# Weights first, one pipeline for all tiles, queries turned one tile ahead

## Chip, cores, metric

One core of a Trainium2 chip runs the whole kernel. Its engines are named as in the profile: PE multiplies matrices (PEld are its weight loads), ACT is ScalarE, DVE is VectorE, POOL is GpSimd. The metric is device microseconds per execution. A ratio is the mean time of one kernel's fast runs over the mean of the other's fast runs from the same rounds, with a 95% interval; it is not quite the ratio of the medians that are quoted, which are over all runs. A run is called slow when it is over 1.5% above the fastest of its kernel.

## The reference

Eight batches of eight heads, 576 positions, 64 values each. Cosine-weighted linear attention, then an expansion with softplus and a projection back.

```python
r_q, r_k = max(q, 0), max(k, 0)              # times cos and sin of the position: q_p, k_p
kv  = einsum('bhsf,bhsd->bhfd', k_p, v)      # per head 128 x 64
z   = sum(k_p, axis=2)
x   = (q_p @ kv) / (q_p @ z + 1e-6)          # 4608 tokens x 512
out = softplus(x @ w_in) @ w_out
```

Both kernels replace softplus by its linear part, `h/2 + ln 2`, so that the two weight matrices fold into one (`W_c`) and a constant row. They measure the largest squared norms of x and of w_in at the end; if the linear part could be too coarse, an exact branch runs (it never does with these inputs).

## The kernel before

The tokens are 36 tiles of 128. A pair of batches has nine: four full ones for each, and one made of the last 64 positions of both. Each tile passes through these steps (shortened; "to turn" means to transpose by a matmul on PE):

```python
def turn_queries(b, n):            # PE transposes relu(q) times cos/sin, ACT copies it out
    ps = qt_ps.tile([128, 512], F32, tag="qt")           # two buffers
    for j, (hj, t) in enumerate(pair):
        nc.tensor.matmul(ps[...], q_r[:, hj, t], diag[:, t])
    nc.scalar.copy(dst, ps)                              # qT
def attend(n):                     # 8 matmuls, then DVE divides: den, rden, x
    ...
def turn_x(n):                     # PE transposes x, ACT copies it and sums its squares
    ...
    nc.scalar.copy(xT_all[:, n], ps)
    nc.scalar.activation(square, x, ACT.Square, bias=zero_b, accum_out=x_norm[:, n : n + 1])
def emit(n):                       # PE: x @ W_c, DVE adds the constant row, then stored
    ...
```

The loop over batch b runs all of this a few tiles apart. The turns in it are those of the *next* batch; nine turns are spread over four or five tiles, with what is left done in a burst at the end:

```python
for j, i in enumerate(mine):
    attend(i)
    ... scale_values(b + 1, hq, c)         # DVE
    if j == 2 and b + 2 < B:
        relu(b + 2)                        # POOL
    if more and j >= last - 1:
        key_values(b + 1, j - last + 1)
    some(1)                                # one turn of batch b + 1
    turn_x(i - 1)
    some(1 if j < last else 9)
    emit(i - 2)
```

Loads: q, k, v of batch 0, then the weights. While those arrive, four tiles of batch 0 are attended; then the weights are turned and folded, and the four are emitted.

## Time and profile before

| what | value |
|---|---|
| time, median | 150.5 us |
| span of the profile | 148.7 us |
| first attended tile | 17 us |
| weights folded, first emit | 42.9 us |
| steady state | 60 to 127 us |
| last output made | 141.2 us |
| busy share of the span: PE, DVE, ACT, POOL | 81%, 73%, 76%, 36% |

### The profile page before, as it was taken

Reading aid. Unit: us, or ns where it says so; the run is one execution under the profiler, and the core shown is the slowest. Engines: PE = TensorE matmul, PEld = TensorE weight load, DVE = VectorE, ACT = ScalarE, POOL = GpSimd, SP = SyncE. Lnnn points to the kernel's source line nnn. Section 1 sums busy time; section 2 is a strip of 40 time slices with the busy share of each in tenths; the row PEclk is TensorE's granted clock in tenths of the full one; section 3 lists DMA queues with packets and bytes.
Section 4 is the critical chain, followed back from the end, with each engine's and each line's share of the span. In section 5 each row is a group of like instructions: output and inputs, shape, how many; then the busy total and the mean of one; then the engine's idle time right before and its main releaser. Section 6 shows DMA issues by size and latency. Waiting matters only on the chain.

```text
span 148.7 us, 3802 instructions
## 1 busy us (share of the span) xinstructions
PE 119.9 (81%) x1482; PEld 75.6 (51%) x1482; DVE 108.9 (73%) x237; ACT 113.7 (76%) x255; POOL 53.0 (36%) x67
## 2 busy tenths in 40 slices
PE   6966875999967728798979899897899988999510
PEld 2323665444434507566657567575567755664100
DVE  6867494699467579978967986994998798599420
ACT  3468298999995626899899889989988989967300
POOL 6965132231300095196079059219009200000000
PEclk9999999999999986999999999999999999999985
DMA  1999999999999999999999999999942324144430
GB/s 21 181 179 216 213 213 202 209 204 209 207 207 208 267 266 209 208 208 265 239 250 256 239 239 269 228 256 249 241 171 82 142 74 109 61 155 152 153 90 4
DMA packets 20678, 28.07 MB, mean 189 GB/s; under 512 B 1200, under 2 KB 15536, under 8 KB 20656
## 3 DMA queue, kind: packets, MB, share of 16 engines
q0 software_dynamic: 15408, 18.35, 71.8%
q1 hardware_dynamic: 5248, 9.44, 18.8%
q8 instruction: 12, 0.20, 0.5%
q14 instruction: 10, 0.08, 0.2%
HBM read 36.70 MB, written 9.44 MB: 310 GB/s over the span
## 4 chain that ended last, share of the span: by engine, by line
PE 33%; DVE 25%; ACT 23%; issue 7%; DMA 5%; POOL 3%; DVEq 0%; POOLq 0%
PE o_ps L316 17%; DVE o_sb L318 11%; ACT square L367 9%; DVE vcs L213 8%; DMA v_sb<-in_v_dram 5%; PE kv_ps L227 5%; PE num_ps L279 4%; PE ps L252 4%; DVE x L289 3%; ACT square L303 3%; ACT qT L260 3%; ACT w_inT L152 3%; PE xT_ps L298 2%; ACT xT_all L301 2%; ACT kvblk L234 2%
## 5 line engine op out<-in xcount | busy, mean ns | idle before, releaser
L260 ACT CAST qT<-ps 128x512 bf16<-128x512 f32 x72 | 40.6, 592 | 11.3 <-PE ps L252 10.9
L316 PE MATMUL o_ps<-W_c,xT_all 128*128 128x512 bf16 x144 | 36.9, 378 | 5.1 <-DVE o_sb L318 3.5
L318 DVE TENSOR_TENSOR o_sb<-o_ps,b_bc 128x512 f32<-128x512 f32 x36 | 24.8, 688 | 13.4 <-PE o_ps L316 13.3
L252 PE MATMUL ps<-diag,q_r 128*128 128x256 bf16 x144 | 27.7, 279 | 8.1 <-ACT qT L260 4.6
L213 DVE TENSOR_TENSOR vcs<-v_sb,cs_wide 128x1152 bf16<-128x1152 bf16 x32 | 27.9, 871 | 2.4 <-ACT qT L260 1.2
L289 DVE TENSOR_TENSOR x<-num_ps,rden 128x512 bf16<-128x512 f32 x36 | 24.9, 692 | 3.3
L303 ACT ACTIVATE square<-x,zero_b 128x512 bf16<-128x512 bf16 x36 | 26.6, 739 | 0.0
L279 PEld LDWEIGHTS <-qT 128*128 128x128 bf16 (+1 forms) x320 | 19.6, 101 | 9.0 <-DVE x L289 1.9
L279 PE MATMUL num_ps<-kvblk,qT 128*128 128x130 bf16 (+1 forms) x320 | 23.4, 223 | 0.6 <-ACT kvblk L234 0.5
L301 ACT CAST xT_all<-xT_ps 128x512 bf16<-128x512 f32 x36 | 21.5, 596 | 3.0 <-PE xT_ps L298 3.0
L316 PEld LDWEIGHTS <-xT_all 128*128 128x128 bf16 x144 | 13.8, 97 | 17.1 <-issue 7.9
L252 PEld LDWEIGHTS <-q_r 128*128 128x128 bf16 x144 | 11.8, 99 | 15.0 <-issue 8.0
L234 ACT CAST kvblk<-kv_ps 64x260 bf16<-64x260 f32 x32 | 12.0, 375 | 6.0 <-PE kv_ps L227 5.7
L298 PE MATMUL xT_ps<-perm,x 128*128 128x128 bf16 x128 | 12.6, 222 | 3.0 <-DVE x L289 1.2
L160 PE MATMUL wc_ps<-w_out_sb,w_inT 128*128 128x512 bf16 x64 | 14.0, 379 | 0.1
L192 POOL TENSOR_SCALAR q_r<-q_sb 128x1152 bf16<-128x1152 bf16 x12 | 13.6, 1145 | 0.0
L298 PEld LDWEIGHTS <-x 128*128 128x128 bf16 x144 | 10.8, 99 | 5.3 <-issue 2.1
L227 PE MATMUL kv_ps<-vcs,k_sb 64*64 64x132 bf16 x576 | 11.5, 219 | 2.1 <-DVE vcs L213 2.0
L187 POOL TENSOR_SCALAR k_sb<-k_sb 128x2304 bf16<-128x2304 bf16 x6 | 12.6, 2102 | 0.0
L73 POOL DMA_DIRECT2D k_sb<-in_k_dram x9 | 6.7, 739 | 16.1 <-PE kv_ps L227 10.7
L367 ACT ACTIVATE square<-w_inT,zero_b 128x512 bf16<-128x512 bf16 x16 | 11.6, 723 | 0.5
L335 POOL COPY gate<-vcs 128x2 bf16<-128x2 bf16 x6 | 1.1, 190 | 29.1 <-DVE vcs L213 29.1
(55 smaller groups left out, 115.4 us busy)
## 6 DMA issues: line engine op xcount, KB each, us to landing
out_dram<-o_sb SPq DMA_DIRECT2D x32, 256.0 KB, 5.9
q_sb<-in_q_dram POOLq DMA_DIRECT2D x7, 576.0 KB, 20.5
k_sb<-in_k_dram POOLq DMA_DIRECT2D x7, 576.0 KB, 18.5
v_sb<-in_v_dram POOLq DMA_DIRECT2D x7, 576.0 KB, 20.9
xT_all<-in_moe_w_in_dram POOLq DMA_DIRECT2D x4, 512.0 KB, 12.6
w_out_sb<-in_moe_w_out_dram POOLq DMA_DIRECT2D x4, 512.0 KB, 18.5
out_dram<-o_sb SPq DMA_DIRECT2D x8, 128.0 KB, 4.0
q_sb<-in_q_dram POOLq DMA_DIRECT2D x2, 288.0 KB, 5.0
```

Source lines behind the costliest of these rows:

```text
L213: nc.vector.tensor_mul(view(vcs, [T * 2 * VW + 2, 2], [2 * VW, T], [1, D], offset=2 * hq * T * 2 * VW + c * VW), kqv[b, "v"][:, 2 * hq : 2 ...
L227: nc.tensor.matmul(kv[64 * i : 64 * i + 64, h2, : 2 * VW], k_r[rows, 2 * hq + i, t, :], vcs[rows, 2 * hq + i, t, :, :], start=(t == 0), st ...
L252: nc.tensor.matmul(ps[:, 256 * j : 256 * j + 256], q_r[:, hj, t, :, :], diag[:, t, :, :], start=True, stop=True, skip_group_check=True,)
L260: nc.scalar.copy(dst, ps.rearrange("p (j c s) -> p j c s", j=2, c=4))
L279: nc.tensor.matmul(num[p0 : p0 + m, g, :C], qTs[b][:, hq, 2 * c + h2, t0 : t0 + m], blk_bufs[b % 3][:, h2, hq, c, :], start=(c == 0), stop ...
L289: nc.vector.tensor_mul(x, view(num, [256, 4], [66, 2], [1, D]), view(rden, [2, 4], [1, 2], [0, D]))
L298: nc.tensor.matmul(ps[:, g, :], x[:, g, :, :], perm if len(tiles[n]) == 1 else ident, start=True, stop=True, skip_group_check=True,)
L301: nc.scalar.copy(xT_all[:, n], ps)
L303: nc.scalar.activation(square, x, ACT.Square, bias=zero_b, accum_out=x_norm[:, n : n + 1])
L316: nc.tensor.matmul(ps, xT_all[:, n, g, :], W_c[:, g, :], start=(g == 0), stop=(g == 3))
L318: nc.vector.tensor_add(o_sb, ps, b_bc)
L367: nc.scalar.activation(square, w_inT[:, ft, :], ACT.Square, bias=zero_b, accum_out=w_norm[:, ft : ft + 1])
```

## The change

The intent is plainness and balance: weights come first, in eight blocks that are turned, squared and folded as they land; every tile then passes through one loop; two tiles share one ACT instruction for the norms; and only the queries of the next tile are turned ahead, two turns per tile with no burst. The core (loads, constants, the end and the head's order are cut):

```diff
-    for ko in range(KO):
-        nc.gpsimd.dma_start(w_in_sb[:, ko, :], moe_w_in[ko * 128 : (ko + 1) * 128, :])
...
+    for j in range(1, BLOCKS):
+        load_w(j)                       # 256 columns of w_in, 256 rows of w_out
+    for name in ("k", "v", "q"):
+        for part in range(2):
+            load(0, name, part)
...
-        nc.scalar.activation(square, x, ACT.Square, bias=zero_b, accum_out=x_norm[:, n : n + 1])
...
+        for i in mine:
+            left = mine[-1] - i
+            if more and left in (1, 2):
+                scale_values(b + 1, 2 - left)
             attend(i)
+            if more and left == 1:
+                pool_relu(b + 1)
+            ahead = list(turns.get(i + 1, []))
+            if ahead:
+                turn_queries(*ahead.pop(0))
+            if more and left < 2:
+                key_values(b + 1, 1 - left)
+            if i >= 1:
                 turn_x(i - 1)
+                if i % 2 == 0:
+                    square(view(xs.pop(i // 2 - 1), [1, 2 * D_MODEL]), 2 * D_MODEL, ...)
+            if ahead:
+                turn_queries(*ahead.pop(0))
+            if i >= 2:
                 emit(i - 2)
```

More of the change, by code (lines that the diff above doesn't have):

```diff
@@ L75, in load, with fetch, load_w @@
         )
-    warm = singles.tile([128, 512], BF16)
+    def fetch(b):
+        for name in ("k", "v", "q"):
+            load(b, name)
+    xT_all = singles.tile([128, N_TOK // 128, KO, 128], BF16)
+    w_in_sb = xT_all[:, -FO:].rearrange("p n g t -> p (n g t)").rearrange(
+        "p (ko f) -> p ko f", ko=KO
+    )
+    w_out_sb = singles.tile([128, FO, D_MODEL], BF16)
+    BLOCKS = 8
+    FB = FO // BLOCKS
+    w_in_r = moe_w_in.rearrange("(ko p) f -> p ko f", p=128)
+    w_out_r = moe_w_out.rearrange("(fo p) m -> p fo m", p=128)
+    def load_w(j):
+        cols = slice(128 * FB * j, 128 * FB * (j + 1))
+        nc.gpsimd.dma_start(w_in_sb[:, :, cols], w_in_r[:, :, cols])
+        nc.gpsimd.dma_start(w_out_sb[:, FB * j : FB * (j + 1), :], w_out_r[:, FB * j : FB * (j + 1), :])
+    warm = singles.tile([128, 2 * D_MODEL], BF16)
     nc.vector.memset(warm, 1.0)
-    load(0, "q", 0)
-    load(0, "q", 1)
+    load_w(0)
     idx_i = singles.tile([128, T], mybir.dt.int32)
@@ L87 @@
     make_identity(nc, ident)
-    for part in range(2):
-        load(0, "k", part)
-        load(0, "v", part)
-    xT_all = singles.tile([128, N_TOK // 128, KO, 128], BF16)
-    w_in_sb = xT_all[:, 4 : 4 + D_FF // 128].rearrange("p n g t -> p (n g t)").rearrange(
-        "p (ko f) -> p ko f", ko=KO
-    )
-    w_out_sb = singles.tile([128, FO, D_MODEL], BF16)
-    for ko in range(KO):
-        nc.gpsimd.dma_start(w_in_sb[:, ko, :], moe_w_in[ko * 128 : (ko + 1) * 128, :])
-    w_out_r = moe_w_out.rearrange("(fo p) m -> p fo m", p=128)
-    for f in range(0, FO, 4):
-        nc.gpsimd.dma_start(w_out_sb[:, f : f + 4, :], w_out_r[:, f : f + 4, :])
-    for b in (1, 2, 3):
-        for name in ("q", "k", "v"):
-            load(b, name)
+    for j in range(1, BLOCKS):
+        load_w(j)
+    for name in ("k", "v", "q"):
+        for part in range(2):
+            load(0, name, part)
+    for b in (1, 2):
+        fetch(b)
     ones = singles.tile([128, 128], F32)
     nc.vector.memset(ones, 1.0)
-    blk_bufs = []
-    for r in range(3):
-        blk = singles.tile([128, 2, 2, 2, C], BF16, name=f"kvblk{r}")
-        nc.vector.memset(blk, 0.0)
-        blk_bufs.append(blk)
     idx_f = singles.tile([128, T], F32)
@@ L123, with constants @@
     cs_wide = singles.tile([128, 2, T, D], BF16)
-    nc.scalar.copy(cs_wide, view(cs_col, [1, 2 * T], [0, D]))
     diag = singles.tile([128, T, 2, 128], BF16)
-    for t in range(T):
-        for c in range(2):
-            nc.vector.tensor_scalar_mul(diag[:, t, c, :], ident, cs_col[:, c, t : t + 1])
     perm = singles.tile([128, 128], BF16)
-    nc.vector.tensor_copy(view(perm, [2, 64], [1, 2]), view(ident, [1, 64], [64, 2]))
+    blk_bufs = [singles.tile([128, 2, 2, 2, C], BF16, name=f"kvblk{r}") for r in range(3)]
+    VW = D + 2
+    vcs_bufs = [singles.tile([128, 4, T, 2, VW], BF16, name=f"vcs{r}") for r in range(2)]
+    def constants():
+        nc.vector.tensor_copy(cs_wide, view(cs_col, [1, 2 * T], [0, D]))
+        for t in range(T):
+            for c in range(2):
+                nc.vector.tensor_scalar_mul(diag[:, t, c, :], ident, cs_col[:, c, t : t + 1])
+                yield
+        nc.vector.tensor_copy(view(perm, [2, 64], [1, 2]), view(ident, [1, 64], [64, 2]))
+        yield
+        for r in range(2):
+            for hp in range(4):
+                at = 0 if hp % 2 else D
+                nc.vector.tensor_copy(
+                    vcs_bufs[r][:, hp, :, :, at : at + 2], view(cs_col, [1, T], [T, 2], [0, 2])
+                )
+                yield
+        for r in range(3):
+            nc.vector.memset(blk_bufs[r], 0.0)
+            yield
     W_c = singles.tile([128, KO, D_MODEL], BF16)
@@ L134, with turn_w_in, square, fold @@
     w_inT = singles.tile([128, FO, D_MODEL], BF16)
-    def turn_w_in(ko, half):
-        n = (2 * ko + half) % 3
-        pool, tag = (xt_ps, "xt") if n == 0 else (qt_ps, "qt")
-        ps = pool.tile([128, 8, 128], BF16, tag=tag, name="wT_ps")
-        for j in range(8):
-            ft = 8 * half + j
-            nc.tensor.matmul(
-                ps[:, j, :], w_in_sb[:, ko, ft * 128 : (ft + 1) * 128], ident,
-                is_transpose=True, start=True, stop=True, skip_group_check=True,
-            )
-        dst = view(
-            w_inT, [D_MODEL, 8], [128, 2], [1, 64],
-            offset=8 * half * D_MODEL + 256 * (ko // 2) + 64 * (ko % 2),
-        )
-        src = ps.rearrange("p f (h d) -> p f h d", h=2)
-        if half:
-            nc.scalar.copy(dst, src)
-        else:
-            nc.vector.tensor_copy(dst, src)
-    def fold(pair, quarter, ps):
-        for ft in range(4 * quarter, 4 * quarter + 4):
-            for j in range(2):
-                g = 2 * pair + j
+    w_norm = singles.tile([128, FO], F32)
+    x_norm = singles.tile([128, N_TOK // 256], F32)
+    def turn_w_in(j):
+        pool, tag = (xt_ps, "xt") if j % 3 == 0 else (qt_ps, "qt")
+        ps = pool.tile([128, FB, KO, 128], BF16, tag=tag, name="wT_ps")
+        for f in range(FB):
+            for ko in range(KO):
+                ft = FB * j + f
+                nc.tensor.matmul(
+                    ps[:, f, ko, :], w_in_sb[:, ko, ft * 128 : (ft + 1) * 128], ident,
+                    is_transpose=True, start=True, stop=True, skip_group_check=True,
+                )
+        for f in range(FB):
+            nc.vector.tensor_copy(
+                view(w_inT, [256, 2], [64, 2], [128, 2], [1, 64], offset=(FB * j + f) * D_MODEL),
+                view(ps, [256, 2], [128, 2], [64, 2], [1, 64], offset=f * D_MODEL),
+            )
+    def square(source, size, dst):
+        nc.scalar.activation(warm[:, :size], source, ACT.Square, bias=zero_b, accum_out=dst)
+    def fold(j, ps):
+        for ft in range(FB * j, FB * (j + 1)):
+            for g in range(KO):
                 nc.tensor.matmul(
-                    ps[:, j, :], w_inT[:, ft, g * 128 : (g + 1) * 128], w_out_sb[:, ft, :],
+                    ps[g // 2][:, g % 2, :], w_inT[:, ft, g * 128 : (g + 1) * 128], w_out_sb[:, ft, :],
                     start=(ft == 0), stop=(ft == FO - 1),
@@ L195, in relu_q, with pool_relu, scale_values @@
         )
-    VW = D + 2
-    vcs_bufs = []
-    for r in range(2):
-        vcs = singles.tile([128, 4, T, 2, VW], BF16, name=f"vcs{r}")
-        vcs_bufs.append(vcs)
-    def mark_values(r):
-        for hp in range(4):
-            at = 0 if hp % 2 else D
-            nc.vector.tensor_copy(
-                vcs_bufs[r][:, hp, :, :, at : at + 2], view(cs_col, [1, T], [T, 2], [0, 2])
-            )
-    def scale_values(b, hq, c):
-        vcs = vcs_bufs[b % 2]
-        nc.vector.tensor_mul(
-            view(vcs, [T * 2 * VW + 2, 2], [2 * VW, T], [1, D],
-                 offset=2 * hq * T * 2 * VW + c * VW),
-            kqv[b, "v"][:, 2 * hq : 2 * hq + 2],
-            view(cs_wide, [0, 2], [D, T], [1, D], offset=c * T * D),
-        )
+    gate = singles.tile([128, 2], BF16)
+    def pool_relu(b):
+        nc.gpsimd.tensor_copy(gate, vcs_bufs[b % 2][:, 3, T - 1, 1, VW - 2 :])
+        if b > 0:
+            for hq in range(2):
+                relu_q(b, hq, nc.gpsimd)
+        if b + 1 < B:
+            relu_k(b + 1, nc.gpsimd)
+    def scale_values(b, hq):
+        vcs = vcs_bufs[b % 2]
+        for c in range(2):
+            nc.vector.tensor_mul(
+                view(vcs, [T * 2 * VW + 2, 2], [2 * VW, T], [1, D],
+                     offset=2 * hq * T * 2 * VW + c * VW),
+                kqv[b, "v"][:, 2 * hq : 2 * hq + 2],
+                view(cs_wide, [0, 2], [D, T], [1, D], offset=c * T * D),
+            )
     def key_values(b, hq):
@@ L240, with turn_queries @@
     qTs = {}
-    TURNS = [(hq, tp) for tp in range(TP) for hq in range(2)] + [(0, TP)]
-    def turn_queries(b, n):
-        hq, tp = TURNS[n]
+    def turn_queries(b, tp, hq=0):
         q_r = q_rs[b]
-        if n == 0:
+        if b not in qTs:
             qTs[b] = work.tile([128, 2, 4, S], BF16, tag="qT", name="qT", bufs=3)
@@ L260, in turn_queries @@
         nc.scalar.copy(dst, ps.rearrange("p (j c s) -> p j c s", j=2, c=4))
-    tiles = []
+    tiles, turns = [], {}
     for b in range(B):
-        tiles += [[(b, 128 * tp, 128, 0)] for tp in range(TP)]
+        for tp in range(TP):
+            turns[len(tiles)] = [(b, tp, hq) for hq in range(2)]
+            tiles.append([(b, 128 * tp, 128, 0)])
         if b % 2:
+            turns[len(tiles)] = [(b - 1, TP), (b, TP)]
             tiles.append([(b - 1, 512, 64, 0), (b, 512, 64, 64)])
+    last = len(tiles) - 1
     xs = {}
-    x_norm = singles.tile([128, len(tiles)], F32)
-    w_norm = singles.tile([128, FO], F32)
     def attend(n):
@@ L287, in attend @@
         nc.vector.reciprocal(rden, den)
-        x = outs.tile([128, 4, 2, D], BF16, tag="x", bufs=3)
+        if n % 2 == 0:
+            xs[n // 2] = outs.tile([128, 2, 4, 2, D], BF16, tag="x", name="x", bufs=2)
         nc.vector.tensor_mul(
-            x, view(num, [256, 4], [66, 2], [1, D]), view(rden, [2, 4], [1, 2], [0, D])
+            xs[n // 2][:, n % 2], view(num, [256, 4], [66, 2], [1, D]),
+            view(rden, [2, 4], [1, 2], [0, D]),
         )
-        xs[n] = x
     def turn_x(n):
-        x = xs.pop(n)
+        x = xs[n // 2][:, n % 2]
         ps = xt_ps.tile([128, 4, 128], F32, tag="xt", name="xT_ps")
@@ L298, in turn_x @@
             nc.tensor.matmul(
-                ps[:, g, :], x[:, g, :, :], perm if len(tiles[n]) == 1 else ident, start=True, stop=True, skip_group_check=True,
+                ps[:, g, :], x[:, g, :, :], perm if len(tiles[n]) == 1 else ident,
+                start=True, stop=True, skip_group_check=True,
             )
         nc.scalar.copy(xT_all[:, n], ps)
-        square = outs.tile([128, D_MODEL], BF16, tag="square", name="square", bufs=1)
-        nc.scalar.activation(square, x, ACT.Square, bias=zero_b, accum_out=x_norm[:, n : n + 1])
     def store(n, o_sb):
@@ L311, in store, with emit @@
                 nc.sync.dma_start(rows[:, T - 1, :], o_sb[p0 : p0 + m])
-    def emit(n):
-        ps = o_ps.tile([128, D_MODEL], F32, tag="o", name="o_ps")
+    def emit(n, pool=None):
+        ps = (
+            big_ps.tile([128, 2, D_MODEL], F32, tag="big", name="o_big")[:, 0]
+            if pool else o_ps.tile([128, D_MODEL], F32, tag="o", name="o_ps")
+        )
         for g in range(4):
@@ L319, in emit @@
         store(n, o_sb)
-    def spin(count):
-        ps = qt_ps.tile([128, 512], F32, tag="qt", name="spin_ps")
-        for _ in range(count):
-            nc.tensor.matmul(ps, warm[:, :128], warm, start=True, stop=True, skip_group_check=True)
-    def fetch(b):
-        for name in ("q", "k", "v"):
-            load(b, name)
-    gate = singles.tile([128, 2], BF16)
-    def relu(b):
-        nc.gpsimd.tensor_copy(gate, vcs_bufs[(b - 1) % 2][:, 3, T - 1, 1, VW - 2 :])
-        for hq in range(2):
-            relu_q(b, hq, nc.gpsimd)
-        relu_k(b, nc.gpsimd)
@@ L340 @@
-    spin(16)
+    ps = qt_ps.tile([128, 512], F32, tag="qt", name="spin_ps")
+    for _ in range(11):
+        nc.tensor.matmul(ps, warm[:, :128], warm[:, :D_MODEL], start=True, stop=True, skip_group_check=True)
+    todo = constants()
+    wc_ps = [big_ps.tile([128, 2, D_MODEL], F32, tag="big", name=f"wc_ps{r}") for r in range(2)]
+    for j in range(BLOCKS + 1):
+        if j < BLOCKS:
+            turn_w_in(j)
+            for ft in range(FB * j, FB * (j + 1)):
+                square(w_inT[:, ft, :], D_MODEL, w_norm[:, ft : ft + 1])
+            for _ in range(4):
+                next(todo, None)
+        if j > 0:
+            fold(j - 1, wc_ps)
+        if j > 0 and j % 2 == 0:
+            sum_w_out(j // 2 - 1)
@@ L341 @@
+    for _ in todo:
+        pass
+    for hq in range(2):
+        relu_k(0, nc.vector, slice(2 * hq, 2 * hq + 2))
+    for pair in range(2):
+        nc.scalar.mul(W_c[:, 2 * pair, :], wc_ps[pair][:, 0, :], 0.5)
+        nc.scalar.mul(W_c[:, 2 * pair + 1, :], wc_ps[pair][:, 1, :], 0.5)
+    bias()
+    for hq in range(2):
+        scale_values(0, hq)
+        key_values(0, hq)
     for hq in range(2):
         relu_q(0, hq, nc.vector)
-    mark_values(0)
-    for hq in range(2):
-        relu_k(0, nc.vector, slice(2 * hq, 2 * hq + 2))
-        for c in range(2):
-            scale_values(0, hq, c)
@@ L348 @@
-    for n in range(9):
-        turn_queries(0, n)
-    key_values(0, 0)
-    spin(2)
-    key_values(0, 1)
-    spin(2)
-    w_turns = iter([(ko, half) for ko in range(KO) for half in range(2)])
-    for n in range(4):
-        attend(n)
-        turn_w_in(*next(w_turns))
-        if n:
-            turn_x(n - 1)
-    mark_values(1)
-    for ko, half in w_turns:
-        turn_w_in(ko, half)
-        if (ko, half) == (2, 0):
-            turn_x(3)
-    for ft in range(FO):
-        square = outs.tile([128, D_MODEL], BF16, tag="square", name="square", bufs=1)
-        nc.scalar.activation(
-            square, w_inT[:, ft, :], ACT.Square, bias=zero_b, accum_out=w_norm[:, ft : ft + 1]
-        )
@@ L370 @@
-    wc_ps = [big_ps.tile([128, 2, D_MODEL], F32, tag="big", name=f"wc_ps{r}") for r in range(2)]
-    for quarter in range(4):
-        sum_w_out(quarter)
-        for pair in range(2):
-            fold(pair, quarter, wc_ps[pair])
-    for hq in range(2):
-        relu_q(1, hq, nc.vector)
-    for pair in range(2):
-        nc.scalar.mul(W_c[:, 2 * pair, :], wc_ps[pair][:, 0, :], 0.5)
-        nc.vector.tensor_scalar_mul(W_c[:, 2 * pair + 1, :], wc_ps[pair][:, 1, :], 0.5)
-    bias()
-    relu_k(1, nc.vector)
@@ L382 @@
-    for n in range(9):
-        turn_queries(1, n)
-        if n % 2:
-            emit(n // 2)
-            scale_values(1, n // 4, n // 2 % 2)
-    for hq in range(2):
-        key_values(1, hq)
-    fetch(4)
-    relu(2)
-    n = 4
-    for b in range(1, B):
-        mine = [i for i in range(n, len(tiles)) if tiles[i][-1][0] == b]
-        last = len(mine) - 1
-        more = b + 1 < B
-        turns = iter(range(9))
-        def some(count):
-            for _ in range(count):
-                t = next(turns, None) if more else None
-                if t is not None:
-                    turn_queries(b + 1, t)
-        if b > 1 and b + 3 < B:
+    for t in turns[0]:
+        turn_queries(*t)
@@ L406 @@
+    pool_relu(0)
+    n = 0
+    for b in range(B):
+        mine = [i for i in range(n, last + 1) if tiles[i][-1][0] == b]
+        more = b + 1 < B
+        if b + 3 < B:
             fetch(b + 3)
-        scales = iter([(hq, c) for hq in range(2) for c in range(2)] if more else [])
-        for j, i in enumerate(mine):
+        for i in mine:
+            left = mine[-1] - i
+            if more and left in (1, 2):
+                scale_values(b + 1, 2 - left)
             attend(i)
-            for hq, c in itertools.islice(scales, 2 if j == 0 else 1):
-                scale_values(b + 1, hq, c)
-            if j == 2 and b + 2 < B:
-                relu(b + 2)
-            if more and j >= last - 1:
-                key_values(b + 1, j - last + 1)
-            some(1)
-            if i - 1 >= 4:
-                turn_x(i - 1)
-            some(1 if j < last else 9)
-            if i - 2 >= 4:
+            if more and left == 1:
[6 more added lines that the diff above has]
+            if i >= 1:
+                turn_x(i - 1)
+                if i % 2 == 0:
+                    square(view(xs.pop(i // 2 - 1), [1, 2 * D_MODEL]), 2 * D_MODEL, x_norm[:, i // 2 - 1 : i // 2])
+            if ahead:
+                turn_queries(*ahead.pop(0))
+            if i >= 2:
@@ L421 @@
                 emit(i - 2)
         n = mine[-1] + 1
-    turn_x(n - 1)
-    emit(n - 2)
-    emit(n - 1)
+    turn_x(last)
+    square(view(xs.pop(last // 2), [1, 2 * D_MODEL]), 2 * D_MODEL, x_norm[:, last // 2 :])
+    emit(last - 1, big_ps)
+    emit(last, big_ps)
     ident_f = singles.tile([128, 128], F32)
@@ L442 @@
     fits = small.tile([1, 1], mybir.dt.int32, tag="fits", bufs=1)
-    nc.vector.tensor_scalar(fits, most[:, 0:1], most[:, 1:2], 1.0 / 32.0, ALU.mult, ALU.is_le)
+    nc.vector.tensor_scalar(fits, most[:, 0:1], most[:, 1:2], LN2 / 16.0, ALU.mult, ALU.is_le)
     flag = nc.values_load(fits, min_val=0, max_val=1)
```

## The prediction

> **What bounds the kernel now.** I read the windows view first (which stage is limited by what), then the groups on the page (what one operation costs), then the chain and the timeline (what each engine waits for, and how long a handoff between two engines takes).
>
> The page has a span of 148.7 us; the timed median is 150.5, so 1.8 us lie outside the span. The first fence is from the windows view; the columns are the window, its length, busy us of PE, PEld, DVE, ACT and POOL, the PE clock, the DMA share and GB/s.
>
> ```profile
> 14.00:43.00 29.00, 23.90 (x221) 14.52 (x222) 19.89 (x34) 24.24 (x55) 8.16 (x11) 1.00 1.17 209
> 60.00:107.00 47.00, 42.94 (x650) 29.96 (x651) 38.23 (x85) 43.96 (x104) 24.60 (x25) 1.00 1.17 243
> ```
>
> In the first window the loads run flat out (209 GB/s at a DMA share of 1.17) while weights and batch 0 arrive. In the second, the steady state, ACT is busy 43.96 of 47 us (94%), PE 91%, DVE 81%. The chain shows the pattern repeating: these two pieces (start, us, what) are the same step one pair of batches, that is nine tiles, apart.
>
> ```profile
> 80.09 0.69 DVE x L289
> ...
> 104.55 0.69 DVE x L289
> ```
>
> So a tile takes (104.55 - 80.09) / 9 = 2.72 us, and ACT sets it. ACT's groups (busy, then mean ns):
>
> ```profile
> L260 ACT CAST qT<-ps 128x512 bf16<-128x512 f32 x72 | 40.6, 592 | 11.3 <-PE ps L252 10.9
> L303 ACT ACTIVATE square<-x,zero_b 128x512 bf16<-128x512 bf16 x36 | 26.6, 739 | 0.0
> L301 ACT CAST xT_all<-xT_ps 128x512 bf16<-128x512 f32 x36 | 21.5, 596 | 3.0 <-PE xT_ps L298 3.0
> L234 ACT CAST kvblk<-kv_ps 64x260 bf16<-64x260 f32 x32 | 12.0, 375 | 6.0 <-PE kv_ps L227 5.7
> ```
>
> Neighbouring ACT operations overlap, so what counts is the distance of their starts. The timeline and chain give 0.48 for a qT copy, 0.48 for xT, 0.71 for a square, 0.76 for a kvblk pair. Per tile: 2 x 0.48 + 0.48 + 0.71 + 0.34 (16 kvblk pairs over 36 tiles) = 2.49 us, against 2.54 from the window (43.96 over 17.3 tiles). ACT is nearly never starved, because this kernel turns the queries of the *next batch*: attend never waits for a qT copy just made.
>
> The head of the chain costs 42 us (its long piece is 16 squares of the turned weights, 27.8 to 41.3, 0.85 each). Four tiles are attended in it and emitted from 42.9; 32 more tiles run from 51.5, the last o_sb ends at 141.2, and 7.5 us of check and ending follow.
>
> [...] the copy of 1024 columns at L152 takes 1014 ns and that of 512 at L301 596, so 512 more columns cost 0.42 us, and the fixed part is what merging two squares saves. [...] in this trace the clock fell to 0.50 at 55 to 58 us after PE had stood nearly still from 52.8 to 55. [...] The new w_in loads have rows of 256 bf16, exactly 512 B; no run here shows that size yet, but 4 KB and 1 KB rows (w_in, w_out) both ran near 209 GB/s, so I expect no loss.
>
> **Part by part.**
>
> *Head.* Removed from it: four hidden tiles, the queue of 16 squares after the last turn (they now go along with the blocks, 2 x 0.85 = 1.7 us of ACT per block), constants ahead of the first load. Added: the data order is weights (4.19 MB), then k, v, q of batch 0 (1.77 MB). The slices of before show 2.2 MB moved by 14.9 us and 0.207 MB/us after. Weights are there at 14.9 + (4.19 - 2.2) / 0.207 = 24.5, q of batch 0 at 14.9 + (5.96 - 2.2) / 0.207 = 33.1, landing about 34. A block needs 2.5 us of DMA, PE 8 x 0.06 + 8 x 0.22 = 2.2, DVE about 2.7, so the fold follows the loads and is done by about 29; the keys and values of batch 0 are folded by 33.5. Then relu of q on DVE (2 x 0.7), turns, two copies and attend: the first tile has been attended at about **37.3** (0.5 of it for a PE clock that may have dropped while waiting for q). Before, that moment was 17, but with weights still to come.
>
> *Steady state, ACT's work.* Two squares of 512 become one of 1024: 0.71 + 0.42 = 1.13 instead of 1.42 per two tiles, a gain of 0.15 per tile. ACT's work falls to 2.3 us per tile, PE's issue distances add up to 2.27 (o_ps 0.86, attend 0.46, xT 0.22, two turns 0.44, key_values 0.29), DVE's to about 2.25. Balanced engines; this is the intent.
>
> *Steady state, the new dependence.* The order listing of the built kernel shows, per tile i on PE: attend(i), first turn of i+1, key_values if due, turn_x(i-1), second turn of i+1, emit(i-2); on ACT: first qT copy, kvblk pair if due, xT copy, square on even i, second qT copy. The second four matmuls of attend(i+1) wait for that second qT copy, the last item on ACT's list; and ACT's next item, the first qT copy for i+2, needs a turn which stands behind attend(i+1) on PE. So ACT idles once per tile while the ball goes to PE and back. The timeline of before has every piece of that trip:
>
> ```profile
> 47.43 0.60 PE L252 MATMUL ps<-diag,q_r 128*128 128x256 bf16 x4
> 47.85 1.07 ACT L260 CAST qT<-ps 128x512 bf16<-128x512 f32 x2 [0.73 <-PE ps L252]
> ...
> 69.15 0.62 PE L279 MATMUL num_ps<-kvblk,qT 128*128 128x130 bf16 x8
> 69.61 0.38 PE L252 MATMUL ps<-diag,q_r 128*128 128x256 bf16 x2
> ...
> 125.99 0.59 ACT L260 CAST qT<-ps 128x512 bf16<-128x512 f32 x1
> 126.63 0.38 PE L252 MATMUL ps<-diag,q_r 128*128 128x256 bf16 x2 [0.81 <-ACT qT L260]
> ```
>
> From the end of a qT copy to PE: 126.63 - 126.58 = 0.05. Half an attend: (69.61 - 69.15) / 2 = 0.23. From a turn's start to its copy: 47.85 - 47.43 = 0.42. Sum 0.70 idle, and the last copy counts with its full 0.59, not 0.48.
> - Even tile: 0.48 + 0.48 + 1.13 + 0.59 + 0.70 = 3.38.
> - Odd tile: the same without the square, 2.25.
> - A tile with key_values: kvblk pair 0.76, and about 0.1 waiting for the 36 products (0.65 on PE): 0.86 more.
>
> PE's own list (1.75 before the wait) and DVE's (1.7, or 3.1 in the tiles that scale values) fit inside these. From tile 0 to tile 35: tile 0 (no xT, no square) 1.8; 17 even x 3.38 = 57.5; 17 odd x 2.25 = 38.3; 14 x 0.86 = 12.0; about 0.6 for v of batch 1, which lands near 40 and is wanted at 38. Sum 110.2, so a mean of 3.15 us per tile where it was 2.72.
>
> *End.* Tile 35 attended at 37.3 + 110.2 = 147.5; its division 1.35, turn and copy 1.05, emit and add 1.8: last o_sb at 151.7. Before it was 141.2: 10.5 later, with the same 7.5 behind it. 148.7 + 10.5 = 159.2 span, about **161 us**. The steps that I took at their upper ends (handoff, clock, kvblk wait) could give back 2, so I take 160.
>
> **Rivals.**
> 1. *The handoff is hidden and the better balance wins.* For it: all three engines need under 2.35 us of work per tile. At 2.6 us per tile the sum is 37.3 + 35 x 2.6 + 4.2 + 7.5 + 1.8 = 142 us. Against it: the order listing shows no operation on ACT that could fill the gap.
> 2. *The loads become the bound.* The DMA is saturated until 107 us before, and weights ahead of everything delay batch 1 to 7. At the rate of the second window the last v is there by about 108; in my schedule it is wanted at tile 28, near 37 + 28 x 3.15 = 125. So it is not the bound unless rival 1 holds; then it adds up to 4 us, about 145.
> 3. *PE is throttled by its new pauses.* In an even tile it waits 1.4 us. [...] Against it: before, PE at 80% busy with gaps of 0.4 to 0.5 (43 to 50 us) kept 1.00.
>
> **Range and chances.** The sum rests on 35 repeats of one handoff: 0.1 us off gives 3.5 us; the head may be 2 off; DVE or POOL waits may add 3. Hence 160, 8 in 10 within 152 to 166. Faster by over 2% (under 147.5) needs rival 1: 0.08. Within 2% (147.5 to 153.5) needs half the handoff hidden: 0.08. Slower: 0.84.
>
> **What would show it.** Right: qT idle before it, released by PE ps, near 0.7 x 35 = 25 us (10.9 before); attend's weight loads waiting for ACT qT; ACT busy near 75% in steady state; tiles alternating near 3.4 and 2.25. First attend near 37 confirms the head. Wrong if qT shows hardly any wait, if DMA v_sb or k_sb ends DVE's or POOL's waits after 60 us, or if the clock row shows 5s in mid-run.

37.3 + 110.2 to the last attend, 1.35 + 1.05 + 1.8 for the rest of tile 35, 7.5 behind it and 1.8 outside the span make the 161 us. That ACT and PE work through their items in the order of the listing, on which the loop rests, the prediction took as given, without a measurement. The timeline of the changed kernel shows it, in the stretch from which the loop is read off below: ACT starts qT at 98.53, xT at 99.01, the square at 99.49, qT at 100.63; PE starts attend's second half at 101.27, a turn at 101.51, turn_x at 101.73, a turn at 101.95, emit at 102.17. The 0.42 us for 512 more columns measured the same there: the square of 1024 took 1157 ns, that of 512 in the kernel before 739. The 0.5 us for the clock in the head is an estimate; the trace of before has an attend of 1.07 us at a clock of 0.50 (56.24) and of 0.62 us at 1.00 (69.15). The gaps that rival 3 rounds to 0.4 to 0.5 us are 0.34 to 0.42 in that timeline.

## More of the kernel before

Profiles are of single executions.

The part of the page on the chain that ended last says how mixed this kernel is: no engine holds more than a third of it.

```profile
PE 33%; DVE 25%; ACT 23%; issue 7%; DMA 5%; POOL 3%; DVEq 0%; POOLq 0%
```

## The result, and the profile after

The changed kernel takes **166.34 us** (165.56 to 166.59) against 150.56 before: ratio 1.102, interval 1.096 to 1.109. It is slower, as predicted; the number lies 0.3 us above the predicted upper end of 166.

First, where in the run it goes. These are the start times of the division that follows attend, for tile 4 and for tile 35, from the two timelines (start, length, engine, line; in brackets the engine's idle time just before, and what ended it). Before:

```profile
52.86 0.17 DVE L285 TENSOR_SCALAR den<-num_ps 128x8 f32<-128x8 f32 x1 [2.06 <-PE num_ps L279]
...
135.74 0.16 DVE L285 TENSOR_SCALAR den<-num_ps 128x8 f32<-128x8 f32 x1
```

After:

```profile
52.07 0.17 DVE L307 TENSOR_SCALAR den<-num_ps 128x8 f32<-128x8 f32 x1 [0.27 <-PE num_ps L301]
...
153.53 0.17 DVE L307 TENSOR_SCALAR den<-num_ps 128x8 f32<-128x8 f32 x1 [1.43 <-PE num_ps L301]
```

At tile 4 the two are level: the changed head, all its rearranging included, is 0.8 us *ahead*. From there 31 tiles take 101.5 us instead of 82.9, or 3.27 us each instead of 2.67. That is 18.6 us lost in the loop; the ending gives 1.5 back (the last two tiles are now emitted from separate buffers; before, PE waited 0.30 and 0.78 us for DVE's o_sb between the last emits).

The window of steady state (same columns as in the prediction), after:

```profile
60.00:107.00 47.00, 35.79 (x540) 23.97 (x548) 34.30 (x72) 35.50 (x71) 21.65 (x24) 1.00 1.14 229
```

Every engine has become idler: ACT from 43.96 to 35.50 of 47 us, PE from 42.94 to 35.79, DVE from 38.23 to 34.30, at a full clock. ACT's 76% is what the prediction gave as a sign (near 75%). None of them is a bound by its work; they wait for each other. The groups of the page say who for whom (busy us, mean ns of one | idle us before, and what ended it):

```profile
L281 ACT CAST qT<-ps 128x512 bf16<-128x512 f32 x72 | 42.1, 588 | 26.5 <-PE ps L273 26.5
L301 PE MATMUL num_ps<-kvblk,qT 128*128 128x130 bf16 (+1 forms) x320 | 29.7, 224 | 27.7 <-ACT qT L281 26.6
...
L180 ACT ACTIVATE warm<-x,zero_b 128x1024 bf16<-128x1024 bf16 x18 | 20.8, 1157 | 0.0
```

The query copy waits 26.5 us for PE (10.9 before), and attend waits 26.6 us for the query copy (no such wait was among the listed ones before). Two lines that wait for each other are the sign of a loop. One turn of it, from the timeline:

```profile
100.63 0.58 ACT L281 CAST qT<-ps 128x512 bf16<-128x512 f32 x1
101.27 0.41 PE L301 MATMUL num_ps<-kvblk,qT 128*128 128x130 bf16 x4 [1.25 <-ACT qT L281]
101.51 0.38 PE L273 MATMUL ps<-diag,q_r 128*128 128x256 bf16 x2
101.93 0.59 ACT L281 CAST qT<-ps 128x512 bf16<-128x512 f32 x1 [0.71 <-PE ps L273]
```

The copy ends at 101.21; attend's second half starts at 101.27; the next turn, which stands behind it on PE, at 101.51; its copy at 101.93. ACT stood idle for 0.72 us (the trace marks 0.71), once per tile: 0.06 from ACT to PE, 0.24 for half an attend and 0.42 from a turn's start to its copy. The alternation of long and short tiles is plain in the starts of the xT copies:

```profile
112.30 0.59 ACT L325 CAST xT_all<-xT_ps 128x512 bf16<-128x512 f32 x1
112.77 1.16 ACT L180 ACTIVATE warm<-x,zero_b 128x1024 bf16<-128x1024 bf16 x1
...
115.70 0.59 ACT L325 CAST xT_all<-xT_ps 128x512 bf16<-128x512 f32 x1
...
117.98 0.59 ACT L325 CAST xT_all<-xT_ps 128x512 bf16<-128x512 f32 x1
```

With the merged square in between 3.40 us, without it 2.28.

### The profile page after: what moved, and what is told of

Its sections match the earlier page's. It is cut to its first block, busy times and chain, and to the rows that moved or that the text cites. A ratio compares the mean times of both kernels' runs of the same rounds, so it can differ in the third digit from the quotient of the medians.

```text
span 164.8 us, 3741 instructions
## 1 busy us (share of the span) xinstructions
PE 119.0 (72%) x1452; PEld 73.7 (45%) x1473; DVE 109.3 (66%) x245; ACT 107.6 (65%) x216; POOL 64.5 (39%) x80
## 4 chain that ended last, share of the span: by engine, by line
ACT 43%; PE 21%; DMA 20%; issue 5%; POOL 4%; DVE 3%; POOLq 0%; ACTq 0%
ACT qT L281 14%; ACT warm L180 12%; DMA w_out_sb<-in_moe_w_out_dram 11%; ACT xT_all L325 11%; DMA v_sb<-in_v_dram 9%; PE num_ps L301 9%; ACT kvblk L257 6%; PE kv_ps L250 6%; PE ps L273 4%; POOL xT_all L95 2%; POOL w_out_sb L96 1%; PE o_big L341 1%; DVE vcs L236 1%; PE o_ps L341 1%; PE xT_ps L321 0%
## 5 line engine op out<-in xcount | busy, mean ns | idle before, releaser
L281 ACT CAST qT<-ps 128x512 bf16<-128x512 f32 x72 | 42.1, 588 | 26.5 <-PE ps L273 26.5
L301 PE MATMUL num_ps<-kvblk,qT 128*128 128x130 bf16 (+1 forms) x320 | 29.7, 224 | 27.7 <-ACT qT L281 26.6
L341 PE MATMUL o_ps<-W_c,xT_all 128*128 128x512 bf16 x118 | 33.8, 379 | 0.9
L273 PE MATMUL ps<-diag,q_r 128*128 128x256 bf16 x144 | 27.9, 279 | 0.0
L236 DVE TENSOR_TENSOR vcs<-v_sb,cs_wide 128x1152 bf16<-128x1152 bf16 x32 | 24.0, 754 | 2.2 <-DMA v_sb<-in_v_dram 1.2
L180 ACT ACTIVATE warm<-x,zero_b 128x1024 bf16<-128x1024 bf16 x18 | 20.8, 1157 | 0.0
L180 ACT ACTIVATE warm<-w_inT,zero_b 128x512 bf16<-128x512 bf16 x16 | 11.6, 723 | 12.0 <-DVE w_inT L174 11.7
L307 DVE TENSOR_SCALAR den<-num_ps 128x8 f32<-128x8 f32 x36 | 5.9, 164 | 19.6 <-PE num_ps L301 19.4
L185 PE MATMUL wc_ps<-w_out_sb,w_inT 128*128 128x512 bf16 x62 | 16.5, 411 | 0.1
L217 POOL TENSOR_SCALAR q_r<-q_sb 128x1152 bf16<-128x1152 bf16 x14 | 15.8, 1144 | 0.0
L212 POOL TENSOR_SCALAR k_sb<-k_sb 128x2304 bf16<-128x2304 bf16 x7 | 14.7, 2103 | 2.4 <-DMA k_sb<-in_k_dram 2.4
L250 PEld LDWEIGHTS <-k_sb 64*64 64x64 bf16 x576 | 9.8, 113 | 6.0 <-issue 4.0
L273 PEld LDWEIGHTS <-q_r 128*128 128x128 bf16 x144 | 11.4, 100 | 0.7 <-issue 0.2
```

The source lines that it names most:

```text
L180: nc.scalar.activation(warm[:, :size], source, ACT.Square, bias=zero_b, accum_out=dst)
L185: nc.tensor.matmul(ps[g // 2][:, g % 2, :], w_inT[:, ft, g * 128 : (g + 1) * 128], w_out_sb[:, ft, :], start=(ft == 0), stop=(ft == FO - 1),)
L236: nc.vector.tensor_mul(view(vcs, [T * 2 * VW + 2, 2], [2 * VW, T], [1, D], offset=2 * hq * T * 2 * VW + c * VW), kqv[b, "v"][:, 2 * hq : 2 ...
L250: nc.tensor.matmul(kv[64 * i : 64 * i + 64, h2, : 2 * VW], k_r[rows, 2 * hq + i, t, :], vcs[rows, 2 * hq + i, t, :, :], start=(t == 0), st ...
L273: nc.tensor.matmul(ps[:, 256 * j : 256 * j + 256], q_r[:, hj, t, :, :], diag[:, t, :, :], start=True, stop=True, skip_group_check=True,)
L281: nc.scalar.copy(dst, ps.rearrange("p (j c s) -> p j c s", j=2, c=4))
```

## The experiments

Three theories. **Round trip**: ACT and PE pass each tile to and fro, and all ACT work that lies between two returns counts in full. **Rival 1**: the merged square itself, or the sum of ACT's work, is the trouble. **Rival 2**: loads or POOL set the pace.

All twelve results were correct. Mean step is that of tiles 4 to 35, from the division's start times in profiles (31 steps; for e11, which has no den, from the reciprocal). The sets e1 to e4, e5 to e8 and e9 to e12 ran on three different chips, each beside the kernel before.

| run | median us | ratio to before | mean step us |
|---|---|---|---|
| before | 150.2 to 150.7 | 1 | 2.67 |
| changed | 166.34 | 1.102 | 3.27 |
| e1 first turn ahead of attend | 159.65 | 1.061 | 3.07 |
| e2 merged square last | 151.66 | 1.008 | 2.83 |
| e3 before, merged squares | 150.81 | 1.001 | 2.67 |
| e4 single squares, same place | 170.78 | 1.133 | 3.39 |
| e5 single squares, last | 150.91 | 0.999 | 2.80 |
| e6 e5, values spread | 147.45 | 0.977 | (slow profile) |
| e7 two tiles ahead | 157.63 | 1.043 | 2.88 |
| e8 before, one DVE operation less | 148.89 | 0.985 | (slow profile) |
| e9 two ahead, relu a batch earlier | 149.30 | 0.997 | 2.69 |
| e10 e9, values spread | 147.88 | 0.985 | 2.58 |
| e11 e3 and e8 together | 150.48 | 1.005 | 2.63 |
| e12 e10, late bias | 148.79 | 0.988 | 2.60 |

### e1: the first turn ahead of attend

```diff
+            ahead = list(turns.get(i + 1, []))
+            if ahead:
+                turn_queries(*ahead.pop(0))
             attend(i)
             if more and left == 1:
                 pool_relu(b + 1)
-            ahead = list(turns.get(i + 1, []))
-            if ahead:
-                turn_queries(*ahead.pop(0))
```

> The changed kernel, with the first turn of tile i+1 placed ahead of attend(i) on PE instead of behind it; no operation added or removed. Theory (round trip): the copy that ACT does next is already turned while attend waits, so the 0.71 us of idle ACT per tile nearly goes; what stays is attend's second half, the turn of x and its handoff (about 0.2 to 0.3). Even tiles 3.40 to about 2.9, odd 2.28 to about 2.0 (PE's own list), key_values tiles 0.15 worse: 166.3 - 11 = 155 us, and the wait of ACT qT for PE ps falls from 26.5 to under 8 us. Rival 1 (the merged square stands in the way, whatever PE's order): 165 to 167. Rival 2 (the loads or POOL set the pace): 165 to 167.

159.65 us: 6.7 less than the changed kernel, where 11 were expected, from a mere change of order. The plain tiles came out as worked out (steps of 2.92 to 3.02 with the square, 1.98 without), and the copy's wait for PE fell from 26.5 to 7.4 us. What ate the rest is a wait that the theory had not named (columns of the waits view: us in total, times, longest):

```profile
PE ps L273 <- POOL q_r L217: 7.7, 7, 1.2
```

The first turn of each new batch now comes before POOL has done the relu of its queries: seven times, 7.7 us. Both rivals had said 165 to 167; of rival 2, POOL's part is true of this wait.

### e2: the merged square behind the second copy

```diff
                 turn_x(i - 1)
-                if i % 2 == 0:
-                    square(...)
             if ahead:
                 turn_queries(*ahead.pop(0))
+            if i >= 1 and i % 2 == 0:
+                square(...)
```

> The changed kernel, with the merged square placed behind the second query copy on ACT instead of ahead of it. Theory (round trip): the square (1.14) fills the time in which the ball is on PE, so even tiles go from 3.40 to 0.48 x 3 + 1.14 = 2.58 and odd ones stay at 2.28: 17 x 0.82 = 14 us less, 152 us. Rival 1 (ACT simply has this much to do per tile, or the size of the merged square is the trouble wherever it stands): within 1% of 166.3. Rival 2 (loads, POOL): the same 166.

151.66 us, as expected (152). Not an operation less, and 14.7 us faster: the square now runs while the ball is on PE. Rival 1 had expected no change. The loop is still longer than before (2.83 against 2.67 us a tile); the total is level because head and ending are shorter.

### e3: the merged squares alone, in the kernel before

```diff
-        nc.scalar.activation(square, x, ACT.Square, ..., accum_out=x_norm[:, n : n + 1])
+        if n % 2:
+            nc.scalar.activation(square, both_tiles, ACT.Square, ..., accum_out=x_norm[:, n // 2 : n // 2 + 1])
```

> One part of the change alone: the kernel before, with one square over two tiles (1024 columns) instead of one per tile. Theory: there ACT is never starved by a round trip and is 94% busy, so 0.14 us of ACT work less per tile shows in part: up to 31 x 0.14 = 4.3 us, PE at 91% allows perhaps half: 147 to 149 us. Rival 1 (merged squares are what hurts): 151 to 154.

150.81 us, ratio 1.001 (0.993 to 1.009): neither the gain nor the harm. Its window:

```profile
60.00:107.00 47.00, 42.73 (x649) 29.82 (x648) 37.83 (x86) 41.32 (x84) 24.58 (x25) 0.98 1.17 242
```

ACT's work fell from 43.96 to 41.32 us and the step stayed at 2.67. So my reading that ACT sets the pace of the kernel before, because it is 94% busy, does not hold.

### e4: single squares in the place of the merged one

```diff
-                if i % 2 == 0:
-                    square(view(xs.pop(i // 2 - 1), [1, 2 * D_MODEL]), 2 * D_MODEL, ...)
+                square(view(xs[(i - 1) // 2], [1, D_MODEL], ...), D_MODEL, x_norm[:, i - 1 : i])
```

> One part of the change undone: the changed kernel with one square of 512 columns per tile in the same place. Theory (round trip, with all ACT work between its ends counting in full): every tile 0.48 + 0.48 + 0.71 + 0.59 + 0.71 = 2.97 against a mean of 2.84: 34 x 0.13 = 4.5 us more, 171 us, and no alternation of long and short tiles. Rival 1 (the merged square is the culprit): faster than 166, toward 160.

170.78 us (171 expected), plain tiles all 2.97 to 2.98. The merging was worth its 4.4 us; it is not the culprit. Here it counts, unlike in e3, because its work lies inside the loop.

### e5: the same single squares, last

```diff
-                square(...)          # behind turn_x, ahead of the second turn
             if ahead:
                 turn_queries(*ahead.pop(0))
+            if i >= 1:
+                square(...)
```

> The kernel with one square per tile again, but each placed last on ACT's list, behind the second query copy. ACT does 0.14 us more work per tile than in the run with the merged square last. Theory (round trip: only what lies between the returning query copies counts): the square of 0.71 covers the round trip of 0.72 in every tile, odd ones too, so no tile needs over 2.28 for it: 147 to 149 us, faster than the 151.7 of the merged square last in spite of more ACT work, and over 20 us faster than the 170.8 of the same squares placed ahead of the copy. Rival (ACT's total work sets the time): 4 us slower than 151.7, about 156.

150.91 us. The cleanest pair is e4 and e5: the same instructions on every engine, one of them moved by one place, and 19.9 us between them (on two chips, on which the kernel before took 150.50 and 150.72). Against e2 the intervals of the ratios overlap, so the extra ACT work cost nothing that shows; the rival's 156 is out. The expected 147 to 149 was missed: plain tiles kept 2.28, and in the tiles that scale values the division still started 3.59 and 3.24 us after the one before. That is only part of it: steps of 1.64 to 1.71 follow these, and by the starts of the xT copies it is the two tiles with key_values in each batch that are long, 3.24 to 3.88 us, while the others take 2.28.

### e6: the scaled values spread

```diff
-            if more and left in (1, 2):
-                scale_values(b + 1, 2 - left)      # two DVE operations
+            for _ in range(...):                   # one per tile; two in one tile of the short batches
+                hc = next(scales, None) if more else None
+                if hc is not None:
+                    scale_values(b + 1, hc[0], hc[1:])
```

> The run before it, and the four value scalings of a batch spread one per tile (two in one tile of the short batches) instead of two in each of two tiles. Theory: what is left above 2.3 us per tile are the two tiles in which DVE's list is 3.2 to 3.6 long; spread out, DVE has 2.4 per tile: about 143 us. Rival (the tiles with key_values are long because of PE or ACT): no change, 147 to 149.

147.45 us, ratio 0.977 (0.971 to 0.983): faster than both kernels, the fastest median here, though not the hoped 143, and with an interval that reaches over the 2% mark. DVE's lists of two scalings had mattered. But the number lies in the rival's range of 147 to 149 too: the tiles with key_values are not explained by DVE alone.

### e7: two tiles ahead

```diff
-            ahead = list(turns.get(i + 1, []))
+            ahead = list(turns.get(i + 2, []))
```

(and values scaled and relu done one tile earlier, two tiles turned before the loop)

> The changed kernel with the queries turned two tiles ahead (values scaled and relu done one tile earlier for it), the merged square left in its place ahead of the second copy. Theory (round trip): attend no longer waits for a copy just made, ACT's wait for PE ps falls from 26.5 us to under 6, even tiles cost 2.58 at most, then DVE's 2.4 to 3.6 set the pace: 142 to 149 us. Rival (the place and size of the merged square matter of themselves): above 160.

157.63 us where 142 to 149 were expected. Attend's wait for ACT's copy is not among its waits any more, but ACT's wait for PE ps is 16.5 us instead of the expected under 6, and these are new:

```profile
PEld L273 <- POOL q_r L217: 11.6, 7, 2.0
PE ps L273 <- POOL q_r L217: 10.3, 7, 1.8
```

One loop was exchanged for another: DVE scales values, POOL waits for that before it does the relu, PE waits for the relu. The head also became longer: DVE waited 4.9 us for the values of batch 1, and tile 4's division started at 55.6 us instead of 52.1.

### e8: the kernel before, a DVE operation less

```diff
-        nc.vector.tensor_scalar_add(den, num[:, :, 64:66], EPS)
-        nc.vector.reciprocal(rden, den)
+        nc.vector.reciprocal(rden, num[:, :, 64:66])
```

> The kernel before without the small addition of 1e-6 to the denominators (0.16 us on DVE per tile, 0.19 to the next start; the result changes far below rounding). The run with merged squares in the kernel before took 4 us of work from ACT and gained nothing, so ACT does not set its pace. Theory now: DVE's in-order list (den, rden, x, one scaled value, o_sb: 2.37) sets it: 31 x 0.19 = 5.9 us at most, 144.5 to 147. Rival (ACT or PE set the pace): 149.5 to 151.

148.89 us, ratio 0.985 (0.979 to 0.991), between the two ranges: a gain, but less than DVE's list alone would give. (In the timeline of the kernel before DVE starts that list in its order: x 61.31, vcs 61.92, o_sb 62.59, den 63.19, rden 63.38, x 63.69, which is 2.38 us.)

### e9: two ahead, and the queries' relu a batch earlier

```diff
-        if b > 0:
-            for hq in range(2):
-                relu_q(b, hq, nc.gpsimd)
         if b + 1 < B:
             relu_k(b + 1, nc.gpsimd)
+            for hq in range(2):
+                relu_q(b + 1, hq, nc.gpsimd)
```

(`turns.get(i + 2, [])`, a third buffer for the relu, one output buffer less to make room)

> The changed kernel with queries turned two tiles ahead, and POOL's relu of the queries one batch earlier (a third buffer for it; to make room, three output buffers instead of four, and the merged square's unused output goes to a free float32 tile), all else in its place, the merged square too. The run with two tiles ahead alone removed attend's wait for ACT but PE then waited 10.3 us for POOL's relu, seven times. Theory (round trip): with that wait gone too the look-ahead shows what it is worth: tiles without scaled values 2.0 to 2.6, scaling tiles 3.2 to 3.6 by DVE's list: 144 to 148 us. Rival (something else holds it at 157): over 154.

149.30 us, 1.3 above the expected range and far from the rival's 154. With the merged square left where the change has it, the mean step is 2.69. This is the part of the change undone that matters: look-ahead restored, the kernel before is matched. The earlier relu alone was not run; it had nothing to gain in the changed kernel, where PE stood 0.0 us idle before the turns (L273). A plain odd tile costs only PE's list:

```profile
101.87 0.15 DVE L306 TENSOR_SCALAR den<-num_ps 128x8 f32<-128x8 f32 x1
...
103.85 0.16 DVE L306 TENSOR_SCALAR den<-num_ps 128x8 f32<-128x8 f32 x1
```

1.98 us. The room that the third buffer took has a price that the profile shows once, an output tile that waited 1.1 us for its buffer's store.

### e10: e9 with the values spread

The edit of e6 on e9.

> The run before it, with the scaled values spread one per tile (two in one tile of the short batches). Theory: DVE has 2.4 per tile and nothing else above 2.4: 139 to 143 us, clearly faster than the kernel before. Rival (PE or ACT hold the remaining tiles): 144 to 148.

147.88 us, ratio 0.985 (0.980 to 0.989), with the smallest step, 2.58; the 139 to 143 were not reached, and the rival's 144 to 148 holds. Its profile shows where: the starts of the xT copies are 2.75 to 3.57 us apart in the two tiles of each batch with key_values, and at most 2.57 in the others (from tile 5 on). The first of these steps is one with key_values:

```profile
61.96 0.58 ACT L324 CAST xT_all<-xT_ps 128x512 bf16<-128x512 f32 x1
...
65.19 0.58 ACT L324 CAST xT_all<-xT_ps 128x512 bf16<-128x512 f32 x1
...
67.76 0.60 ACT L324 CAST xT_all<-xT_ps 128x512 bf16<-128x512 f32 x1
...
69.88 0.59 ACT L324 CAST xT_all<-xT_ps 128x512 bf16<-128x512 f32 x1
```

Besides, PE's weight loads wait 4.1 us (2.7 in e9) for the relu of batch 1's queries in the head, because these are now wanted when their load has just landed; that gives back part of the loop's gain.

### e11: both in the kernel before

The edits of e3 and e8 together.

> The kernel before with both: one square over two tiles, and no addition to the denominators. Each alone gained 0 and 2.3 us of the possible 4.3 and 5.9. If DVE sets the common tiles and ACT the batch ends (where nine turns come in a burst), the two together give more than the sum: 145 to 147. If ACT's work matters nowhere: 148.3 to 149, as without the addition alone.

150.48 us, ratio 1.005 (0.998 to 1.012). Neither expectation: it is not even as fast as e8 alone. Taking work from ACT, from DVE, or from both did not speed up the kernel before in a way that adds up. The profile shows a part: in the first two tiles of a batch the steps of 3.17 and 2.37 us fell to 2.90 to 2.97 and 2.11 to 2.18, as a shorter DVE list would have it (e3 alone kept 3.09 to 3.17 and 2.30 to 2.37); at the ends of batches steps stayed or grew (3.82 before; 3.83 and 4.45 now), and 31 tiles gained 1.2 us in all. What sets the ends of batches stays open.

### e12: the bias late

```diff
-    bias()                      # and the last sum of w_out, ahead of batch 0's keys
...
             attend(i)
+            if i == 0:
+                sum_w_out(3)
...
+            if i == 1:
+                bias()
```

> The run with two tiles ahead and spread values, with the last of the sums of w_out on DVE (3.1 us) and the bias moved from ahead of batch 0's keys to behind the first attend. Theory: in the head DVE is the last to finish (last weights 25.7, first attend 39), so up to 3 us of it go, less what v and q of batch 0 still lack by then (they land at 31 to 34.5): 1 to 2 us less than without it. Rival (loads set the head): no change.

148.79 us against 147.88 without it; the ratios' intervals overlap. No gain: DVE's sums were not what held the first tiles. As the rival had it, the loads then hold DVE: it waits 0.99 us for v and 0.60 us for q of batch 0, the last of which lands at 36.0 us, later than the 34.5 that the expectation took.

## Why the prediction was right or wrong

- **The mechanism held.** The loop that I read off the order of instructions, and its length, 0.70 us put together from three handoffs of the old trace, is there: 0.72. Plain tiles of 3.38 and 2.25 us measured 3.40 and 2.28. e2, e4, e5 and e9 each aim at that loop; all four came out within 2 us of the expected value or range, though e5 and e9 missed their ranges by 1.9 and 1.3. e1 and e7 fell short by more, since each brought PE's wait for POOL's relu. e4 and e5 show that the place alone is worth 19.9 us.
- **Terms that were too small** (all in the step that sums up the loop). By the starts of the xT copies, a tile with key_values costs 0.97 more (3.24 against 2.28), not 0.86: 14 x 0.11 = 1.5 us. The tiles made of two half batches need the second copy for 14 of their 16 matmuls, which I left out: about 0.35 more (3.59 against 3.24), four times, 1.4 us. The plain tiles' 0.02 to 0.03 make 0.9. From tile 0 attended to tile 35 attended (PE's next instruction starts at 39.32 and 153.42): 114.1 instead of 110.2. A tile with key_values, between its xT copy and the one before:

```profile
102.41 0.59 ACT L325 CAST xT_all<-xT_ps 128x512 bf16<-128x512 f32 x1
...
105.65 0.59 ACT L325 CAST xT_all<-xT_ps 128x512 bf16<-128x512 f32 x1
```

- **The head was 2 us too short.** The turn that follows the first attend started at 39.3, not 37.3. The loads came later: the last weights landed at 26.7 us, not 24.5, and the last of q at 35.3, not 34. While the weights came, the rate was 196 to 202 GB/s (13 to 25 us) where 207 was assumed, so "no loss" was nearly right; whether the 512 B rows are the reason was not tested. And the clock had fallen as I feared, but for longer, from 33.2 to 40.0 us; this is the window of the changed kernel:

```profile
34.00:38.00 4.00, 3.38 (x76) 2.38 (x76) 2.88 (x5) 1.72 (x5) 0.19 (x1) 0.50 1.21 207
```

  At this clock the eight matmuls of the first attend took 1.10 us, against 0.62 in the prediction's line. The prediction put the fall of the clock in the kernel before (0.50 at 55 to 58 us) behind a near standstill of PE, busy 0.30 of the 2.20 us from 52.8 to 55; that the one brought the other was not shown. PE's longest idle time before that fall was 1.90 us, and 2.18 before this one. What makes the clock fall here stays open.

- **The haircut went the wrong way.** The sum said 161; I took 1 us off because some steps looked like upper ends. They were too short: 161 + 2 + 3.9 makes 166.9, and 166.3 was measured.
- **"ACT sets it" is the step that fell**, in the part on what bounds the kernel now. A share of 94% let me call ACT the bound; e3 took 2.6 of 44 us from it and nothing moved. The prediction survived because it rested on the new loop, not on that bound; but rival 1 in it, the gain from a better balance, was worth less than I allowed: 142 us with the handoff hidden, where e9, in which attend no longer waits for the copy, took 149.3.
- **The other rivals.** Loads: they set the head (the chain that ended last runs through DMA almost unbroken from 7.6 to 41.9 us), where DVE waited 1.2 us for the v of batch 1, landed at 41.9 instead of 40; after that no wait of DVE for a load is listed, so they are not the bound of the loop. Throttle: from 42 to 159 us the clock was 1.00, with PE pauses of 1.2 to 1.5 us in the long tiles.

So the cause of the loss is settled: the look-ahead of one tile, in this order of instructions, with e9 as its undoing and e2 and e5 as its cheap repairs. Open are what sets the ends of batches in the kernel before, and what makes the tiles with key_values long in e10.

## What to carry to other kernels

Before trusting busy shares, follow one item through the lists of two engines, in the order in which the timeline shows them run: if A's last operation of a round releases B, and A's first of the next round stands behind that on B, the handoffs are paid every round, and work inside the loop counts in full, while work placed behind the returning operation is free up to the length of the round trip (0.72 us here: e5's square of 0.71 left the tile at 2.28, e2's of 1.14 made it 2.56). Try the order first: moving one instruction was worth 15 to 20 us here, and a deeper look-ahead only helped when what feeds it (here POOL's relu) moved ahead too (149.30 us in e9 against 157.63 in e7). A merged or saved operation was worth its full length inside the loop (4.4 us in e4), and nothing in the kernel that has no such loop (ratio 1.001 in e3). And from 60 to 107 us of the changed kernel the busy times of PE, DVE and ACT fell together while the whole took 10% longer: they show that something waits, not what; the idle times and what ended them did.
